# Attention scores computed in column groups of 32, and streamed weights issued at other steps, in a four-layer prompt kernel

## The chip, the cores and the metric

The kernel runs on one core of one Trainium2 chip. The metric is the device time of one execution in microseconds. The time of the kernel before is the median of three runs.

## The reference

Four layers, A, B, A, B, each added to the residual stream `x` of 2048 tokens by 640 features. Only layer A is touched by the change.

```python
# layer A, on the layer-normed x: 64 segments of 32 tokens, one after the other
mem = mem0                                   # 8 memory rows x 640
for s in range(64):
    h = concat([mem, x[32*s : 32*s+32]])     # 40 rows
    q, k, v = h @ Wq, h @ Wk, h @ Wv         # 32 heads of 192
    scores = q @ k.T * 192**-0.5             # 40 x 40 per head, masked
    p = softmax(scores)
    o = (p @ v) @ Wo                         # back to 40 x 640
    mem = o[:8]                              # carried to the next segment
    outs.append(o[8:])
```

Layer B is a linear attention over all 2048 tokens, with learned feature maps.

## The kernel before

**Segments and rounds.** `A_pre` computes, for all segments at once, what does not depend on the memory: keys, queries and values of the last 8 tokens of each segment, stored in DRAM (`kqb_d`, `vb_d`). `A_chain` then walks the 64 segments in order, since each needs the memory rows of the one before. In a segment the 32 heads are worked off in `NR` = 4 rounds of 8 heads, in rising order in even segments and falling order in odd ones. The instruction order is written out by hand for all engines; nothing is rescheduled. Of the 40 rows of a segment, 32 (8 memory rows and the first 24 tokens) go through the chain's projections, as `hT`, 128 x 5 x 32.

**One round** (`n` is 0 to 3), in TensorE's order: the projection of the queries of the next round (`project`, L1154: five steps over the contraction, each with four matmuls into four 32-column tiles of the array, 32 stationary columns and 384 moving ones); the scores (`scores`, L1191) with the exponential on ScalarE (`weigh`, L1273, into `E`); in round 1 some products with Wo (`wo_round`, L1263); the projection of the next round's keys; `attend` (L1204, `ps_o`) and `attend_tails` (L1217, `ps_t`), which multiply E with the values; in round 2 eight more products with Wo; the projection of the next round's values. After round 3's scores come the rest of the products with Wo, the sum that makes the next `hT` (L1453, L1455), and the next segment.

**The scores.** `QK` holds keys and queries of eight heads as 128 x (2, 8, 80): of the 80 columns 64 belong to the 32 rows of two heads (turned there by VectorE, L1174, from `raws`, which ScalarE fills from PSUM, L1169) and 16 to the last tokens of the two heads (copied in by GpSimd, L1130, from `kqb`). `KT` and `QT` are its two halves. Two matmuls add up to one 80 x 80 block of `S`; a round has four blocks, so eight matmuls, each with 80 stationary columns on the whole array. There is one `QK`, so VectorE and GpSimd write the next round's columns after the scores have read these. Round 3's keys are turned in two halves.

**Streamed weights.** Most of Wq, Wk, Wv and Wo lies in SBUF. Seven pieces of 384 KB (3 of Wq, 2 of Wk, 2 of Wv) are held in slots that two rounds share, and `wo_both`, four pieces of 320 KB, holds rows 4 to 11 of Wo for the first or the last round. After round 0 has used a slot, `project` puts the load that refills it for round 3 into the list `held`; `load_both` adds the four Wo pieces in round 1, the one with rows 4 and 5 last. Round 3 reads rows 6 to 11 first, then 0 to 5. `release` takes the first load from the list and issues it on SP's queue, with a wait on one given matmul, so that few loads are under way at a time. Which matmul that is stands in the table `PACE`: for a projection (`"Q"`, `"K"` or `"V"`, round) the contraction step after which one load is released:

```python
if PACE.get((m, n)) == i:
    self.release(last)
```

Of the kernel before, what the change touches and what calls it, by code (L numbers as in the profile page):

```python
# [22 lines left out]

VH = 194

PACE = {("Q", 0): 0, ("K", 0): 1, ("V", 0): 3, ("Q", 1): 3, ("K", 1): 1, ("V", 1): 1, ("Q", 2): 1, ("K", 2): 3, ("V", 2): 3,
        ("Q", 3): 3, ("K", 3): 3}

STEPS = (2, 6)

# [92 lines left out]
class Kernel:  # L123
# [934 lines left out]
    def A_chain(self, xn_dram, at_dram, li, load_slot, piece, late_wo, load_both, wo, low):  # L1058
        nc, tc, KC, NSEG = self.nc, self.tc, self.KC, self.NSEG
        scale = float(self.Dh) ** -0.5  # L1060
        NR = 4
        with tc.tile_pool(name=f"A{li}_ch", reuse_waits="tile", bufs=1) as sp, \
# [4 lines left out]
            KT, QT = QK[:, 0], QK[:, 1]  # L1067
# [69 lines left out]
            def project(hT, ps, m, n, s, steps):  # L1137
# [3 lines left out]
                for i in steps:  # L1141
# [14 lines left out]
                    if n == 0 and b >= KC - ns:  # L1156
                        self.held.append(lambda b=b: load_slot(m, order[NR - 1], b))
                    if PACE.get((m, n)) == i:
                        self.release(last)
# [25 lines left out]
            def scores():  # L1185

                S = pop.tile([P, 512], F32, name="ps_s", tag="s")
                for x in range(2):
                    for c in range(4):
                        c0 = 160 * x + 80 * (c // 2)  # L1190
                        nc.tensor.matmul(S[0:80, c0:c0 + 80], lhsT=KT[:, 4 * x + c, :], rhs=QT[:, 4 * x + c, :],  # L1191
                                         start=(c % 2 == 0), stop=(c % 2 == 1), skip_group_check=True)
                return S

            pair = [None]
# [72 lines left out]
            def weigh(E_before=None):  # L1268
                S = scores()
                if E_before is not None:  # L1270
                    attend_tails(E_before, 2)
                E = sp.tile([P, 320], BF16, name="E", tag="E")
                nc.scalar.activation(out=E[0:80, 0:320], in_=S[0:80, 0:320], func=ACT.Exp, scale=scale)  # L1273
                return E
# [276 lines left out]
```

## Time and profile before

| | us |
|---|---|
| median of three runs | 3175.91 (3167.55 to 3177.78) |
| profiled execution | 3169.9 |
| its span, first to last instruction | 3168.0 |
| of which the two A chains | about 1189 and 1192 |
| TensorE busy | 2993.8 (95%) |
| VectorE, ScalarE, GpSimd busy | 2184.4, 1906.3, 1392.8 |
| DMA engines' mean busy share within the A chains | 78% |

PE is TensorE's matmuls, PEld its weight loads, DVE VectorE, ACT ScalarE, POOL GpSimd, SP SyncE. L1154 is line 1154 of the kernel. Matmuls are pipelined, and their ends are modelled: a start-to-start distance says more than the length of one. Times are microseconds from the start of the span unless marked ns. The granted TensorE clock was 0.992 of full speed over the span. A row of a group gives line, engine, operation, tiles (out<-in), shape and count, then busy time and mean ns of one, then the idle time ahead of these instructions and what ended most of it; "issue" there means nothing that the profile shows.

### The profile page before, as it was taken

What the parts mean: (1) busy time and instruction counts of PE and PEld (TensorE: products, weight loads), DVE (VectorE), ACT (ScalarE), POOL (GpSimd) and SP (SyncE); (2) the same over time, 40 slices, a digit from 0 to 9 for tenths busy, and PEclk for the clock granted to TensorE, in tenths of its full rate; (3) what the DMA queues carried; (4) which work ended last, traced back from release to release, by engine and by line L of the source; (5) the groups of instructions that cost most, each with busy time, mean ns of one, the idle gap of its engine ahead of it and who ended that gap; (6) DMA issues with size and microseconds to landing.
All of it is one profiled execution on the core that took longest, in us unless ns stands there. A gap on an engine that the chain in (4) does not pass through costs nothing.

```text
span 3168.0 us, 141538 instructions
## 1 busy us (share of the span) xinstructions
PE 2993.8 (95%) x59586; PEld 1920.6 (61%) x59586; DVE 2184.4 (69%) x5426; ACT 1906.3 (60%) x4536; POOL 1392.8 (44%) x2872
## 2 busy tenths in 40 slices
PE   8789999999999999899999999999999999998999
PEld 7656666666666665555377566666666666665553
DVE  5467777777777777656644677777777777776565
ACT  3356666666666666646433566666666666666453
POOL 3255555555555555430122555555555555554300
PEclk9999999999999999999999999999999999999999
DMA  9977777877877877840268777777877777778300
GB/s 377 340 263 257 261 248 251 265 257 250 272 252 251 267 256 246 288 166 1 103 246 320 257 255 246 263 264 245 264 259 249 255 261 255 246 259 287 130 1 34
DMA packets 338873, 749.67 MB, mean 237 GB/s; under 512 B 68874, under 2 KB 115330, under 8 KB 335166
## 3 DMA queue, kind: packets, MB, share of 16 engines
q1 hardware_dynamic: 267998, 636.89, 58.3%
q0 software_dynamic: 69376, 100.10, 10.9%
q8 instruction: 469, 7.68, 1.0%
q10 hardware_dynamic: 864, 3.64, 0.3%
q14 instruction: 166, 1.36, 0.1%
HBM read 670.77 MB, written 78.01 MB: 236 GB/s over the span
## 4 chain that ended last, share of the span: by engine, by line
PE 76%; DVE 8%; DMA 6%; issue 5%; ACT 3%; POOL 2%; ACTq 0%; DVEq 0%; SPq 0%; POOLq 0%
PE ps_qk_k L1154 13%; PE ps_qk_q L1154 13%; PE ps_v L1154 12%; PE ps_w L1263 11%; PE ps_s L1191 6%; PE ps_pre L985 4%; PE ps_o L1204 3%; PE kv L1506 2%; DVE raws L1453 2%; ACT raws L1234 2%; DVE hT L1455 2%; PE ps_pq L517 2%; PE ps_t L1217 1%; PE ps_wo L466 1%; DVE QK L1377 1%
## 5 line engine op out<-in xcount | busy, mean ns | idle before, releaser
L1154 PEld LDWEIGHTS <-hT 128*32 128x32 bf16 x30720 | 787.1, 96 | 461.0 <-DVE hT L1455 78.7
L1174 DVE STREAM_TRANSPOSE QK<-raws 128x512 bf16<-128x512 bf16 (+1 forms) x1152 | 730.0, 642 | 219.3 <-ACT raws L1169 163.7
L1130 POOL COPY QK<-kqb 64x192 bf16<-64x192 bf16 x1024 | 349.5, 341 | 486.6 <-PE ps_s L1191 254.1
L1154 PE MATMUL ps_qk_q<-arena,hT 128*32 128x384 bf16 x10240 | 511.3, 327 | 41.4 <-DVE hT L1455 25.6
L1154 PE MATMUL ps_qk_k<-arena,hT 128*32 128x384 bf16 x10240 | 510.1, 328 | 3.0 <-ACT E L1273 1.4
L1169 ACT ACTIVATE raws<-ps_qk_k 128x512 bf16<-128x512 f32 (+1 forms) x640 | 313.5, 510 | 254.0 <-PE ps_qk_k L1154 243.5
L1234 ACT ACTIVATE raws<-ps_o,under 128x192 bf16<-128x192 f32 x1024 | 373.8, 420 | 121.9 <-DVE under L1228 102.5
L1154 PE MATMUL ps_v<-arena,hT 128*32 128x384 bf16 x8192 | 428.4, 326 | 4.0 <-issue 3.0
L1169 ACT ACTIVATE raws<-ps_qk_q 128x512 bf16<-128x512 f32 x512 | 305.7, 597 | 166.6 <-PE ps_qk_q L1154 153.1
L1134 POOL DMA_DIRECT2D Vp<-vb x512 | 257.9, 504 | 316.6 <-PE ps_t L1217 210.7
L1123 POOL DMA_DIRECT2D kqb<-kqb x512 | 292.4, 571 | 69.7 <-POOL QK L1130 59.4
L1191 PEld LDWEIGHTS <-QK 128*80 128x80 bf16 x4096 | 196.0, 121 | 184.9 <-issue 153.8
L1183 DVE CAST Vp<-ps_v 64x384 bf16<-64x384 f32 x512 | 286.3, 559 | 24.5 <-ACT Vp L1181 8.7
L1263 PE MATMUL ps_w<-arena,under 128*32 128x320 bf16 x6144 | 280.6, 300 | 9.5 <-DMA arena<-wo_rows 4.1
L1191 PE MATMUL ps_s<-QK 128*80 128x80 bf16 x4096 | 253.4, 209 | 21.8 <-POOL QK L1130 13.6
L1181 ACT ACTIVATE Vp<-ps_v 64x384 bf16<-64x384 f32 x512 | 246.4, 481 | 35.1 <-PE ps_v L1154 33.6
L1273 ACT ACTIVATE E<-ps_s 80x320 bf16<-80x320 f32 x512 | 217.7, 425 | 42.8 <-PE ps_t L1217 28.6
L985 PEld LDWEIGHTS <-arena 128*128 128x128 bf16 x1920 | 187.9, 98 | 31.0 <-issue 4.7
L1119 POOL DMA_DIRECT2D attn<-under x128 | 91.3, 713 | 262.0 <-DVE under L1115 223.5
L1112 ACT ACTIVATE raws<-ps_w 64x160 f32<-64x160 f32 x256 | 76.6, 299 | 201.1 <-DVE raws L1453 199.6
L1204 PE MATMUL ps_o<-Vp,E 80*32 80x193 bf16 x4096 | 180.3, 248 | 10.2 <-issue 5.7
L1263 PEld LDWEIGHTS <-under 128*32 128x32 bf16 x6144 | 147.2, 96 | 41.6 <-issue 9.8
(167 smaller groups left out, 4360.5 us busy)
## 6 DMA issues: line engine op xcount, KB each, us to landing
arena<-wo_rows SPq DMA_DIRECT2D x560, 320.0 KB, 4.8
arena<-in_A_Wq_dram SPq DMA_DIRECT2D x427, 384.0 KB, 4.5
arena<-in_A_Wk_dram SPq DMA_DIRECT2D x298, 384.0 KB, 5.6
arena<-in_A_Wv_dram SPq DMA_DIRECT2D x290, 384.0 KB, 5.9
kqb<-kqb POOLq DMA_DIRECT2D x512, 48.0 KB, 4.3
kqb<-arena POOLq DMA_DIRECT2D x14, 1536.0 KB, 9.7
Vp<-vb POOLq DMA_DIRECT2D x512, 24.2 KB, 3.8
otb<-otb POOLq DMA_DIRECT2D x256, 48.0 KB, 4.0
```

Source lines behind the costliest of these rows:

```text
L985: nc.tensor.matmul(ps[:, T * i:T * i + T], lhsT=w[b][:, P * c:P * c + P], rhs=xBT[:, b, :], start=(b == 0), stop=(b == KC - 1))
L1123: nc.gpsimd.dma_start(out=kqb[:], in_=self.kqb_d[r, :, s, :])
L1130: nc.gpsimd.tensor_copy(out=o, in_=kqb[h, :].rearrange("p (x c q) -> p x c q", c=3, q=16))
L1134: nc.gpsimd.dma_start(out=Vs[n % 2][64:80, :], in_=self.vb_d[s // 8, r].rearrange("g (t s) x f -> s (g t) (x f)", s=8)[s % 8])
L1154: last = nc.tensor.matmul(o, lhsT=hT[:, b, :], rhs=rhs, start=(i == 0), stop=(i == KC - 1), tile_position=(0, 32 * g), skip_group_check=True)
L1169: nc.scalar.activation(out=raw[:, c], in_=ps[:, c], func=ACT.Copy)
L1174: nc.vector.transpose(out=o, in_=i)
L1183: nc.vector.tensor_copy(out=o, in_=i)
L1191: nc.tensor.matmul(S[0:80, c0:c0 + 80], lhsT=KT[:, 4 * x + c, :], rhs=QT[:, 4 * x + c, :], start=(c % 2 == 0), stop=(c % 2 == 1), skip_gro ...
L1204: nc.tensor.matmul(O[G][32 * h:32 * h + 32, VH * G:VH * G + 193], lhsT=E[0:80, 80 * h + 32 * G:80 * h + 32 * G + 32], rhs=V[0:80, VH * h:V ...
L1234: nc.scalar.activation(out=out, in_=i, func=ACT.Copy, scale=rc[G])
L1263: step = nc.tensor.matmul(W[q:q + 32, 0:320], lhsT=OT[i // 6][:, i % 6 // 2, 32 * (i % 2):32 * (i % 2) + 32], rhs=rhs, start=(first and i ...
```

## The change

The eight score matmuls of a round become 24: each is cut along its 80 stationary columns (the keys) into groups of 32, 32 and 16, which go to the column tiles 0, 32 and 64 of the array and to the same partitions of `S`. The moving operand, `QT` with 80 columns, and the sums are as before, in all four rounds.

The table `PACE` gets other steps. Eleven loads are released in a segment, in the same order as before; the n-th load moves from one step to another:

| load | released before after | released now after |
|---|---|---|
| 1 to 3, Wq | Q0 step 0, K0 step 1, V0 step 3 | Q0 step 0, K0 step 2, V0 step 4 |
| 4 and 5, Wk | Q1 step 3, K1 step 1 | K1 step 0, V1 step 1 |
| 6 and 7, Wv | V1 step 1, Q2 step 1 | Q2 step 3, K2 step 1 |
| 8 to 11, Wo | K2 step 3, V2 step 3, Q3 step 3, K3 step 3 | V2 step 1, Q3 step 1, K3 step 1, V3 step 2 |

```diff
-PACE = {("Q", 0): 0, ("K", 0): 1, ("V", 0): 3, ("Q", 1): 3, ("K", 1): 1, ("V", 1): 1, ("Q", 2): 1, ("K", 2): 3, ("V", 2): 3,
-        ("Q", 3): 3, ("K", 3): 3}
+PACE = {("Q", 0): 0, ("K", 0): 2, ("V", 0): 4, ("K", 1): 0, ("V", 1): 1, ("Q", 2): 3, ("K", 2): 1, ("V", 2): 1, ("Q", 3): 1,
+        ("K", 3): 1, ("V", 3): 2}
...
                 for x in range(2):
                     for c in range(4):
                         c0 = 160 * x + 80 * (c // 2)
-                        nc.tensor.matmul(S[0:80, c0:c0 + 80], lhsT=KT[:, 4 * x + c, :], rhs=QT[:, 4 * x + c, :],
-                                         start=(c % 2 == 0), stop=(c % 2 == 1), skip_group_check=True)
+                        for g, m in enumerate((32, 32, 16)):
+                            nc.tensor.matmul(S[32 * g:32 * g + m, c0:c0 + 80], lhsT=KT[:, 4 * x + c, 32 * g:32 * g + m],
+                                             rhs=QT[:, 4 * x + c, :], start=(c % 2 == 0), stop=(c % 2 == 1),
+                                             tile_position=(0, 32 * g), skip_group_check=True)
```

## The prediction

> **What bounds the kernel now.** I read the page first, then the groups by line, then TensorE's timeline of one segment, then the timelines of ScalarE and of the weight queue, and last the landings of the weight loads.
>
> ```profile
> PE 2993.8 (95%) x59586; PEld 1920.6 (61%) x59586; DVE 2184.4 (69%) x5426; ACT 1906.3 (60%) x4536; POOL 1392.8 (44%) x2872
> ...
> PE 76%; DVE 8%; DMA 6%; issue 5%; ACT 3%; POOL 2%; ACTq 0%; DVEq 0%; SPq 0%; POOLq 0%
> ```
>
> TensorE is busy 95% and is 76% of the chain that ended last. The stretches table gives two A chains of 1189 and 1192 us: 64 segments of some 18.6 us each, four rounds to a segment, 512 rounds in all. Only these chains change.
>
> ```profile
> L1191 PEld LDWEIGHTS <-QK 128*80 128x80 bf16 x4096 | 196.0, 121 | 184.9 <-issue 153.8
> ...
> L1191 PE MATMUL ps_s<-QK 128*80 128x80 bf16 x4096 | 253.4, 209 | 21.8 <-POOL QK L1130 13.6
> ```
>
> The first group is the scores' weight loads: 153.8 us of idle time ended by nothing that the profile shows, 0.3 us for each of the 512 blocks. TensorE's timeline (start, length, line, tiles, count) shows it inside one round:
>
> ```profile
> 902.25 0.34 PE L1204 MATMUL ps_o<-Vp,E 80*32 80x193 bf16 x8
> 902.42 0.26 PE L1217 MATMUL ps_t<-Vp,E 80*32 80x193 bf16 x4
> 902.50 0.34 PE L1154 MATMUL ps_v<-arena,hT 128*32 128x384 bf16 x4
> ...
> 903.32 0.99 PE L1154 MATMUL ps_qk_q<-arena,hT 128*32 128x384 bf16 x20
> 904.23 0.50 PE L1191 MATMUL ps_s<-QK 128*80 128x80 bf16 x8
> 904.66 0.73 PE L1263 MATMUL ps_w<-arena,under 128*32 128x320 bf16 x16
> ```
>
> A projection of 20 matmuls takes 0.82 us from its start to the next block's (902.50 to 903.32), five groups of four column tiles at 0.163 us. From 903.32 to 904.66 there are 1.34 us, so a score block costs 0.52. In the trace's single instructions the eight 80-column matmuls start 38 ns apart (0.30 us); 0.10 lie ahead of them (first score weight load 0.255 us after the last projection matmul, where the next group comes after 0.152) and 0.10 to 0.14 behind. These gaps stand only where 32-column blocks give way to 80-column ones and back.
>
> **Scores, the block by itself.** 24 matmuls replace 8 (16,384 more matmuls and as many weight loads). Groups of four column tiles take 0.163 us for 384 columns and 0.083 for 193 (902.25 to 902.42 holds two), that is 0.42 ns a column and 2 ns; 80 columns give 0.036 us for the three tiles of a product and 0.29 for eight. The 16-column tile is in the trace too (ps_t, 80*16) and follows 32-column tiles without a gap. So 0.53 becomes 0.29: 0.24 saved per block, 125 us over 512, if TensorE alone set the time. Bounds for a pair of load and matmul: 2 ns an instruction when it is popped from a full queue; 8.8 ns (56 instructions between two semaphore waits 0.49 us apart) if that were the sequencer's pace, which makes 48 instructions 0.42 us. I take the streaming value since tiles of one group start 3.5 ns apart; the other end would cost 0.16 us a segment, 20 us. The densest long stretch here is 12 matmuls in 0.25 us (902.25 to 902.50), 21 ns each.
>
> The Trainium skill, "TensorE: Matmul & The Clock Gate", section "Wait — 56ns, not 53.3ns?", says that start-to-start never falls below about 25 ns however few columns there are; by that the 24 would take 0.60 us, an estimate, and 512 blocks lose some 35 us. Those 21 ns already lie below it. The same page, "Part 3: Packing small matmuls", says that a weight load overlaps matmuls in flight only in another row group; here all loads use the same rows and still cost nothing between projection groups.
>
> **What of it reaches the path.** Per segment, with the waits of the other engines:
> - Round 0: the block cannot start earlier, since its key transposes end 0.15 us ahead of it (VectorE) in nearly every segment. Only the gap behind goes: 0.11.
> - Round 1: VectorE and GpSimd are done 0.4 and 2 us ahead, and ps_w covers the exponential. All of it: 0.24.
> - Round 2: ScalarE runs without a break from the scaled rows to E:
>
> ```profile
> 906.97 0.73 ACT L1234 ACTIVATE raws<-ps_o,under 128x192 bf16<-128x192 f32 x2
> 907.59 0.48 ACT L1181 ACTIVATE Vp<-ps_v 64x384 bf16<-64x384 f32 x1
> 907.96 0.41 ACT L1247 ACTIVATE raws<-ps_t,under 128x192 bf16<-128x192 f32 x1
> 908.26 0.59 ACT L1169 ACTIVATE raws<-ps_qk_q 128x512 bf16<-128x512 f32 x1
> 908.74 0.43 ACT L1273 ACTIVATE E<-ps_s 80x320 bf16<-80x320 f32 x1
> ```
>
> E ends at 909.17 and ps_o of that round starts at 909.26; over all segments ps_o starts 0.14 us after E, where 0.10 is the least seen. Earlier scores do not make E earlier: 0.03 gained, the rest becomes a wait of ps_o on E.
> - Round 3: the second half of the key transposes ends at 910.68, 0.05 after the block has begun; that chain hangs on ps_o of round 2. 0.19 gained.
>
> Sum 0.57 us a segment, 73 us over 128. GpSimd's copies into QK end a median 0.64 us (a tenth under 0.16) before round 3's scores, which now come up to 0.45 earlier: I put 5 us for that, bounds 0 and 15. TensorE's extra instructions cost nothing by themselves while the streaming value holds.
>
> **Streamed weights.** Each segment reloads seven 384 KB slots and four 320 KB pieces. On SP's queue:
>
> ```profile
> 898.02 2.44 SPq L748 DMA_DIRECT2D arena<-in_A_Wq_dram  x3
> 900.95 1.36 SPq L748 DMA_DIRECT2D arena<-in_A_Wk_dram  x2
> 903.05 1.14 SPq L748 DMA_DIRECT2D arena<-in_A_Wv_dram  x2
> 906.09 3.55 SPq L797 DMA_DIRECT2D arena<-wo_rows  x4
> ```
>
> Seven are issued within 5.8 us. Median time to landing by position, from the landing semaphores: 4.03, 4.50, 4.53, 4.97, 5.55, 5.67, 6.09, then 4.72, 4.66, 4.82, 4.37. That is a queue: with the seventh 5.84 after the first, (6.09 - 4.03 + 5.84)/6 = 1.31 us of service for 384 KB and 2.72 fixed; likewise 0.97 and some 2.65 for the pieces. It gives the positions between to 0.25 us.
>
> The order of the eleven stays; the steps move. An issue follows its matmul group by 0.38 us. Counted from the segment's first matmul, with the gains above, the new issues fall at 0.39, 1.53, 2.67, 4.07, 5.30, 6.45, 7.78 and 8.83, 9.65, 10.75, 12.39. The queue then gives 4.50 for the seventh (the last slot of Wv) and 3.66 for the eleventh (the piece with rows 4 and 5, which the last products of the segment read). Their uses come 4.55 and 3.7 us after issue. Before, they came 6.5 and 5.0 after it, with median slacks of 0.69 and 0.64 us; now both are near nothing, while every other load keeps over 0.5. With the spread of those landings (deviation 0.48 us, taken segment by segment from the trace) the mean stall is 0.30 us a segment, 38 us in all. A piece behind a stall in ps_v has that much more time, so the two do not add. Ends: 0.13 us (17 us) if landings come 0.3 sooner, 0.54 (69 us) if 0.3 later. SP's store of vb waits in the same queue behind the eleventh, but for an eviction 3 us later, so it is not delayed.
>
> **Sum.** 73 - 5 - 38 = 30 us. The profiled execution is 3169.9 us with a span of 3168.0; it would come to about 3140. The median of the runs shown is 6 us higher: 3176 - 30 = 3146, and I give 3145.
>
> **Rivals.**
> - *The pace holds* (0.20). Spread issues shorten the landings more than the queue says, and stalls stay at 10 us or less: 3176 - 73 + 5 + 10 = 3118, down to 3085 if round 2's ScalarE chain also gives way. For it: the share of DMA is 78% in the chains, not full. Against: 4.03 us is the landing of a load with no other in front.
> - *The last slot of Wv is late* (0.18, slower). It is released at step 1 of K in round 2, some 1.9 us later than before, and used at step 4 of V in round 3, 4.55 us after issue. If landings stay above 5.1 us, as for positions 5 to 7 now, the 0.57 gained is gone; at 5.55 the stall is 1.0 and the time 3176 + (1.0 - 0.57) x 128 + 5 = 3236; at 5.2, 3190. For it: those landings are in the trace. Against: they were reached with loads 1 us apart, and the new gaps are 1.1 to 1.6.
> - *Issue-bound tiles* (0.10). If 24 pairs go no faster than the 21 ns each seen, a block costs 0.50 and nearly nothing is saved, while looser timing leaves the loads their slack: 3165 to 3185. The skill's 25 ns would make it about 3210.
> - Forecast (0.52): stalls take 10 to 56 us of the 68 left after GpSimd's 5: 3118 to 3164.
>
> **Numbers.** About 0.3%, 10 us, is what a measurement can tell. Faster: 0.50 of the forecast and 0.20 of the first rival, 0.70; slower: 0.17 of the second and 0.04 of the third, 0.21; within it the rest, 0.09. The range 3085 to 3200 takes in the first rival, the third, and the cheap end of the second; left out is a tenth to a fifth.
>
> **What would show it.** Right: score blocks of 24 that take 0.29 us with no gap either side, the idle time of their weight loads gone from 153.8 to under 30 us; waits of ps_o on E in round 2; waits of ps_v and ps_w on DMA of 20 to 60 us in all where now there are 9; Wv landings near 4.5. Wrong: blocks over 0.4 us (issue), or DMA waits over 80 us (the pace), or under 10 (the gain larger).

## The result and the profile after

The changed kernel takes 3276.93 us (median of four runs) where the kernel before took 3174.4 beside it: a ratio of 1.0333, 95% interval 1.0302 to 1.0364. It is 3.3% slower, where 1% faster was forecast. The profiled execution has a span of 3286.7 us, 118.7 longer.

The page after, with the lines that answer to those of before, and the instruction queue's line (packets, MB, share), first as it stands on the page of before:

```profile
q8 instruction: 469, 7.68, 1.0%
```

```profile
PE 2963.5 (90%) x67778; PEld 2041.0 (62%) x67778; DVE 2180.9 (66%) x5426; ACT 1912.5 (58%) x4536; POOL 1397.0 (43%) x2872
...
q8 instruction: 533, 8.73, 1.1%
...
PE 68%; DMA 12%; DVE 8%; issue 6%; ACT 4%; POOL 1%; SPq 0%; DVEq 0%; ACTq 0%; POOLq 0%
...
L1192 PE MATMUL ps_s<-QK 128*32 128x80 bf16 (+1 forms) x12288 | 251.5, 202 | 37.7 <-issue 21.4
L1192 PEld LDWEIGHTS <-QK 128*32 128x32 bf16 (+1 forms) x12288 | 211.1, 96 | 111.0 <-DVE QK L1174 38.2
```

TensorE is busy for less time (2963.5 us against 2993.8) in a longer span, so work was removed and waiting added. The weight loads of the scores no longer wait 153.8 us for nothing (34.7 us of "issue" are left in the waits). The instruction queue moved 533 packets of 16 KB instead of 469; the trace holds 136,485 instructions of TensorE (weight loads, matmuls and waits), 256 for each packet.

TensorE's timeline of a round in which nothing is late shows what the column groups do (line 1192 is the scores):

```profile
396.85 0.99 PE L1154 MATMUL ps_qk_q<-arena,hT 128*32 128x384 bf16 x20
397.67 0.39 PE L1192 MATMUL ps_s<-QK 128*32 128x80 bf16 x18
397.86 0.31 PE L1265 MATMUL ps_w<-arena,under 128*32 128x320 bf16 x1
397.88 0.25 PE L1192 MATMUL ps_s<-QK 128*32 128x80 bf16 x6
397.95 0.72 PE L1265 MATMUL ps_w<-arena,under 128*32 128x320 bf16 x15
```

The scores follow the projection at its usual 0.82 us, and the next block's groups follow 0.28 us later (one matmul of it, for the column tile that the scores leave free, slips in before them). The single instructions show groups of three 35 ns apart. Two rounds on, in the same segment:

```profile
403.73 0.29 PE L1192 MATMUL ps_s<-QK 128*32 128x80 bf16 x9
405.18 0.29 PE L1192 MATMUL ps_s<-QK 128*32 128x80 bf16 x9 [1.16 <-issue]
405.27 0.26 PE L1219 MATMUL ps_t<-Vp,E 80*32 80x193 bf16 x1
405.28 0.25 PE L1192 MATMUL ps_s<-QK 128*32 128x80 bf16 x6
```

After nine of the 24 matmuls TensorE stands still for 1.16 us, and nothing that the profile follows releases it. Among the DMA packets of the trace there is one of the instruction queue, 16 KB, from 402.94 to 403.83: TensorE goes on 1.35 us after it has landed. That is the pattern to look for. Some of TensorE's longest waits (total us, times, longest us), after:

```profile
PE ps_w L1265 <- issue: 71.4, 67, 2.6
PE ps_qk_k L1154 <- issue: 34.5, 37, 2.1
...
PE ps_w L1265 <- DMA arena<-wo_rows: 22.4, 42, 1.6
...
PE ps_s L1192 <- issue: 21.4, 26, 2.3
...
PE ps_v L1154 <- DMA arena<-in_A_Wv_dram: 11.4, 21, 1.9
PE ps_v L1154 <- issue: 10.2, 18, 1.1
```

and the same of before:

```profile
PE ps_w L1263 <- issue: 13.6, 24, 1.5
...
PE ps_w L1263 <- DMA arena<-wo_rows: 8.1, 12, 1.5
...
PE ps_v L1154 <- issue: 3.0, 8, 0.6
...
PE ps_v L1154 <- DMA arena<-in_A_Wv_dram: 0.6, 1, 0.6
```

To compare kernels I counted, in the A chains of each trace, every distance over 0.33 us between successive matmul starts, less the ordinary 0.152. It is a *late instruction fetch* if TensorE resumes 1.15 to 1.65 us after the last packet of the instruction queue ended, a *late weight* if it resumes within 0.06 us of the landing of a streamed load. The window for fetches was set by eye: in the changed kernel the gaps before ps_qk_k lie 1.28 to 1.53 us (10% to 90%) behind the packet. Some gaps are counted there by chance. Those in neither class (some 100 to 135 us in every kernel) are waits for other engines, VectorE most of all.

The last column of the table needs no window. It counts TensorE's instructions from the start of the trace and takes the gaps that begin at one fixed instruction of every 256. In the changed kernel 194 of all 572 gaps begin there, in both chains at position 193; the other gaps are spread over all positions. (Where 18 matmul records are missing from a trace, position 175 of the second chain is the same instruction.) So TensorE stops at the end of the instructions that it holds: these are late fetches, and of the 30 and 15 us that the window gives e5 and e8 most is chance.

| kernel | median us | ratio to before | late fetch, us (times) | late weight, us (times) | stops at the fixed instruction, us (times) |
|---|---|---|---|---|---|
| before | 3172 | | 50 (89) | 27 (31) | 41 (68) |
| changed | 3277 | 1.033 | 207 (221) | 54 (94) | 193 (194) |
| e1 new scores, old steps | 3270 | 1.030 | 222 (254) | 18 (26) | 211 (230) |
| e2 old scores, new steps | 3241 | 1.022 | 39 (73) | 108 (164) | 29 (45) |
| e3 before + empty matmuls, bunched | 3325 | 1.048 | 167 (200) | 11 (18) | 160 (179) |
| e6 before + empty matmuls, spread | 3288 | 1.036 | 107 (164) | 16 (24) | 98 (137) |
| e5 as e1, nothing streamed | 3031 | 0.955 | 30 (75) | 4 (3) | 7 (9) |
| e9 as e1, no Wo pieces streamed | 3192 | 1.006 | 161 (212) | 18 (19) | 147 (166) |
| e8 before, nothing streamed | 3096 | 0.975 | 15 (32) | 2 (5) | 2 (3) |
| e10 new scores in round 0 alone | 3176 | 1.000 | 74 (120) | 29 (35) | 60 (88) |
| e4 new scores in round 1 alone | 3183 | 1.004 | 101 (141) | 22 (29) | 94 (119) |
| e11 new scores in round 3 alone | 3209 | 1.011 | 86 (124) | 29 (37) | 83 (108) |

For the changed kernel the account nearly closes: late fetches +157, late weights +28, and a gain of 65 to 72 us (e8 against e5, below) come to 113 to 120; the span grew by 118.7, the median by 102.5. The granted clock was 0.985 of full speed in this profiled execution against 0.992 before, which is worth 23 us at most (an estimate, as if TensorE's clock set the whole time); e1 loses nearly as much at 0.991.

### The profile page after: what moved, and what is told of

It is laid out like the page before. It is cut to its first block, busy times and chain, and to the rows that moved or that the text cites. A ratio compares the mean times of both kernels' runs of the same rounds, so it can differ in the third digit from the quotient of the medians.

```text
span 3286.7 us, 157795 instructions
## 1 busy us (share of the span) xinstructions
PE 2963.5 (90%) x67778; PEld 2041.0 (62%) x67778; DVE 2180.9 (66%) x5426; ACT 1912.5 (58%) x4536; POOL 1397.0 (43%) x2872
## 4 chain that ended last, share of the span: by engine, by line
PE 68%; DMA 12%; DVE 8%; issue 6%; ACT 4%; POOL 1%; SPq 0%; DVEq 0%; ACTq 0%; POOLq 0%
PE ps_qk_q L1154 12%; PE ps_qk_k L1154 12%; PE ps_v L1154 10%; PE ps_w L1265 9%; DMA arena<-wo_rows 6%; PE ps_pre L985 5%; DMA arena<-in_A_Wv_dram 4%; PE ps_s L1192 4%; PE ps_o L1206 3%; PE kv L1508 2%; DVE raws L1455 2%; ACT raws L1236 2%; PE ps_wo L466 2%; PE ps_pq L517 1%; DVE hT L1457 1%
## 5 line engine op out<-in xcount | busy, mean ns | idle before, releaser
L1154 PEld LDWEIGHTS <-hT 128*32 128x32 bf16 x30720 | 925.9, 97 | 438.9 <-issue 117.2
L1154 PE MATMUL ps_qk_k<-arena,hT 128*32 128x384 bf16 x10240 | 552.2, 328 | 34.8 <-issue 34.5
L1154 PE MATMUL ps_qk_q<-arena,hT 128*32 128x384 bf16 x10240 | 525.3, 329 | 46.5 <-DVE hT L1457 22.8
L1154 PE MATMUL ps_v<-arena,hT 128*32 128x384 bf16 x8192 | 449.0, 327 | 20.4 <-DMA arena<-in_A_Wv_dram 11.4
L1265 PE MATMUL ps_w<-arena,under 128*32 128x320 bf16 x6144 | 310.3, 301 | 36.1 <-issue 31.2
L1192 PE MATMUL ps_s<-QK 128*32 128x80 bf16 (+1 forms) x12288 | 251.5, 202 | 37.7 <-issue 21.4
L1192 PEld LDWEIGHTS <-QK 128*32 128x32 bf16 (+1 forms) x12288 | 211.1, 96 | 111.0 <-DVE QK L1174 38.2
L1265 PEld LDWEIGHTS <-under 128*32 128x32 bf16 x6144 | 187.1, 97 | 47.0 <-issue 40.2
L1206 PE MATMUL ps_o<-Vp,E 80*32 80x193 bf16 x4096 | 195.2, 251 | 16.1 <-issue 5.7
```

The source lines that it names most:

```text
L1154: last = nc.tensor.matmul(o, lhsT=hT[:, b, :], rhs=rhs, start=(i == 0), stop=(i == KC - 1), tile_position=(0, 32 * g), skip_group_check=True)
L1192: nc.tensor.matmul(S[32 * g:32 * g + m, c0:c0 + 80], lhsT=KT[:, 4 * x + c, 32 * g:32 * g + m], rhs=QT[:, 4 * x + c, :], start=(c % 2 == 0) ...
L1206: nc.tensor.matmul(O[G][32 * h:32 * h + 32, VH * G:VH * G + 193], lhsT=E[0:80, 80 * h + 32 * G:80 * h + 32 * G + 32], rhs=V[0:80, VH * h:V ...
L1265: step = nc.tensor.matmul(W[q:q + 32, 0:320], lhsT=OT[i // 6][:, i % 6 // 2, 32 * (i % 2):32 * (i % 2) + 32], rhs=rhs, start=(first and i ...
```

## The experiments

**Each half alone.** Theory A: TensorE runs out of instructions. Theory B: the release steps make the loss. e1 keeps the table of before:

```diff
 PACE = ...            # as before
+                        for g, m in enumerate((32, 32, 16)):   # scores as changed
```

> The new scores with the release steps of the kernel before. Theory A (TensorE runs out of instructions: 16 KB fetches that resume it some 1.4 us after they land, more often since a score block now takes 48 instructions): the fetch-like stalls stay near the 210 us of the changed kernel (52 before), DMA waits near the 17 us of before, and the time is 3240 to 3280. Theory B (the release steps make the loss): fetch-like stalls matter little and the time is about 3100, the 73 us gained.

Measured: 3270.08 us, ratio 1.0301 (1.0276 to 1.0327). A holds: late fetches 222 us, late weights 18. Of its waits:

```profile
PE ps_w L1265 <- issue: 46.5, 61, 1.6
PE ps_s L1192 <- issue: 39.8, 45, 2.3
PE ps_qk_k L1154 <- issue: 35.4, 34, 2.8
...
PE ps_w L1265 <- DMA arena<-wo_rows: 7.9, 11, 1.7
```

e2 is the other half: the new table, with the eight matmuls of 80 columns.

> The scores of before with the new release steps. Theory A: fetch-like stalls stay near 52 us; the eleventh load is used 3.9 us after issue and lands after 4.4, so DMA waits rise by 0.3 to 0.6 us a segment, 40 to 75 us: 3215 to 3250. Theory B: the whole loss is here, and more, since nothing is gained: 3280 or above.

Measured: 3241.04 us, ratio 1.0224 (1.0195 to 1.0254). A's range again, and the release steps are a loss of their own, 2.2%:

```profile
PE ps_w L1263 <- DMA arena<-wo_rows: 52.1, 94, 1.6
...
PE ps_v L1154 <- DMA arena<-in_A_Wv_dram: 21.8, 43, 1.1
```

Late weights rise by 81 us, late fetches do not. B's claim that the whole loss is here is refuted by e1. In the changed kernel the same steps cost only 28 us of late weights, probably because time lost to instructions is time in which weights land.

**Instructions without the scores.** e3 adds 16 matmuls of one moving column behind each unchanged score block, into columns of `S` that nothing reads:

```diff
+                for i in range(16):
+                    g = i % 4
+                    nc.tensor.matmul(S[32 * g:32 * g + 32, 400:401], lhsT=hT[:, 0, :], rhs=hT[:, 0, 0:1],
+                                     start=True, stop=True, tile_position=(0, 32 * g), skip_group_check=True)
```

> The kernel before with 16 added matmuls of one moving column behind each score block, into columns of S that nothing reads: the same number of TensorE instructions as in the changed kernel, no gap removed, release steps of before. Theory A: fetch-like stalls rise from 52 to 150 to 220 us; with 0.04 to 0.1 us of TensorE time a block the kernel takes 3290 to 3400. Theory B: only those 20 to 50 us: 3195 to 3225.

Measured: 3325.01 us, ratio 1.0482 (1.0452 to 1.0512), in theory A's range; late fetches 167 us, and 0.11 us of TensorE's time a block. Instructions that compute nothing bring back three quarters of the added stalls, with no change of the scores or the steps. e6 spreads as many over the projections (65 a segment against 64), and writes unused columns of `ps_w`. Unlike e3's, these matmuls alter the kernel's result, probably because `ps_w` holds sums that are still open; e6 tells of time alone.

> The kernel before with as many empty one-column matmuls as e3 (65 a segment against 64), but spread one or two to a step over the projections instead of 16 behind each score block, into columns of ps_w that nothing reads. If the number of instructions makes the stalls, the fetch-like stalls are 150 us or more, as in e3 (167); if their bunching does, they stay under 100. TensorE's own time for them is open, 15 to 80 us.

Measured: 3287.59 us, ratio 1.0360 (1.0343 to 1.0377), late fetches 107 us. Neither answer holds alone: spread instructions add half the stalls that bunched ones do (57 us against 117), so number and bunching both count.

**Why a fetch is late.** e5 is e1 without the streamed loads of all but the last segment:

```diff
+                if self.dry:          # set in segments 0 to 62: mark the slot, load nothing
+                    return None
```

> As e1 (new scores, release steps of before), but the eleven streamed loads of every segment but the last are left out in both A layers, so round 3 multiplies with the weights that the slots hold already. If instruction fetches come late because weight packets stand ahead of them, the fetch-like stalls fall from 222 us to under 80 and the time to 3090 to 3120. If a fetch simply takes its 2.4 us and is asked for too late for so dense an instruction stream, the stalls stay above 150 us and the time near 3240, lower than e1 by its 18 us of DMA waits and little else.

Measured: 3030.58 us, ratio 0.9551 (0.9534 to 0.9568), late fetches 30 us, only 7 of them at the fixed instruction, with the same 533 fetches. The time is 60 us below its range: the late fetches and weights that went come to 206 of the 240 us, and the rest is not accounted for. So the fetch of 2.4 us is not too slow in itself; it is late when loads of weights are under way. e9 streams the seven slots but not the Wo pieces:

> As e5, but only the four Wo pieces of a segment are left out and the seven 384 KB slots are loaded: two thirds of the streamed bytes. If fetches wait behind the packets of loads, the fetch-like stalls lie between 30 (nothing streamed) and 222 (all), 80 to 160 us, and the time between 3031 and 3270; stalls in the rounds 0 and 1, where the slot loads still are in flight, stay, and those after round 2 go.

Measured: 3191.95 us, ratio 1.0060 (1.0041 to 1.0078), late fetches 161 us, a hair above the expected bound, and only in part where expected. Behind round 3's scores 36 us are left (e1: 86). From round 1's scores to round 3's 126 us stay (e1: 134), and half of these fall after round 2's scores, where they should have gone: 63 us (e1: 72) with a mean 1.0 streamed load under way in place of 4.2.

The traces show why. The fetch of the next 256 instructions never starts sooner than some 20 instructions before TensorE passes the fixed instruction ahead of them, and TensorE stops 256 instructions after that passing if they are not there. Between round 2's scores and round 3's there are only 162 instructions, so a fetch that is missed there was due before, when e9 still has a mean 3.7 loads under way. In e1 the median packet starts 1.1 to 1.3 us after the passing when at most two streamed loads are under way then, 1.6 us with three, 2.3 with four and 2.6 with five; in e5 it is 0.6 us. The packet itself takes 1.0 to 1.1 us each time. Loads under way delay the start of a fetch, not its transfer.

e8 takes the streamed loads from the kernel before, to see the gain of the column groups free of both waits.

> The kernel before with the streamed loads left out as in e5 (scores of 80 columns, release steps of before; round 3 multiplies with the weights that the slots hold). Without waits on loads and with few late fetches the two score forms stand side by side: e5 at 3031, and this one 73 us above it if the columns gain what the traces say, 3095 to 3115. Its own fetch-like stalls should be under 30 us where before has 50.

Measured: 3095.84 us, ratio 0.9751 (0.9724 to 0.9778), late fetches 15 us. e5 stands 65 us below it: that is what the column groups are worth when little else is late. The median segment takes 17.38 us in e5 and 17.94 here, 0.56 less, which makes 72 us over 128.

**Column groups in one round.** `scores` takes the round and cuts only in that one (32 added instructions a segment), with the steps of before:

```diff
-                S = scores()
+                S = scores(n in (1,))      # (0,) in e10, (3,) in e11
```

> Column groups only in round 1, where the whole 0.24 us of a block reaches the path; release steps of before; 32 added instructions a segment instead of 128. Theory A: a gain of 31 us less a quarter of the 158 us of added stalls if they grow in proportion, 3180 or so, 3145 to 3160 if they grow faster than the count. Theory B: 3143.

Measured: 3183.38 us, ratio 1.0043 (1.0026 to 1.0060). It is the 3180 given for theory A with stalls in proportion, not theory B's 3143. Late fetches grew by 52 us for a quarter of the instructions (172 for all of them, in e1), rather more than in proportion, and outweigh the 31 us gained.

> Column groups in round 0 only, release steps of before. In all runs so far hardly any stall falls between round 0's scores and round 1's (3 us of over 200), where few loads are in flight. If the place of the instructions matters, the 14 us that round 0 gains stay and the added stalls are under 10 us: 3160 to 3170, faster than before. If each 16 added matmuls a segment cost their stalls wherever they stand, as in round 1 (52 us), the time is 3195 to 3215.

Measured: 3175.64 us, ratio 1.0002 (0.9989 to 1.0015): no difference. Neither expectation holds. The stalls did not follow in the same round (2 us), but later ones grew: 74 us in all, 24 more, which eats the gain. The reason given for the round was wrong: a mean 4.5 streamed loads are under way between its scores and the next, as many as in the two stretches that follow. But fewer than 256 instructions lie between them (194), so the fetches that could be missed there were due before round 0's scores; behind round 3's scores only 1.4 loads are under way on average.

> The same in round 3 only, where 0.1 to 0.2 us of a block reaches the path (13 to 25 us) and half of the Wo loads are in flight. Stalls of 20 to 50 us added behind round 3's scores: 3175 to 3205, not faster than before.

Measured: 3208.67 us, ratio 1.0111 (1.0094 to 1.0128). Late fetches 86 us, 62 of them behind round 3's scores (29 before). Not faster, as expected, and a little worse than the range.

**Earlier release on the kernel before.** e7 moves the last four releases to step 1:

```diff
-("Q", 2): 1, ("K", 2): 3, ("V", 2): 3, ("Q", 3): 3, ("K", 3): 3
+("Q", 2): 1, ("K", 2): 1, ("V", 2): 1, ("Q", 3): 1, ("K", 3): 1
```

> The kernel before with its last four releases at step 1 instead of step 3 of K and V in round 2 and of Q and K in round 3, 0.33 us earlier each; scores of before. The last Wo piece then has 5.3 us instead of 5.0 to land: DMA waits before ps_w fall from 13 us to under 6, unless the queue takes the difference. 3163 to 3172, at or within what can be told from before.

Measured: 3174.98 us, ratio 1.0002 (0.9988 to 1.0016). No difference, where 3163 to 3172 was expected; the late weights stayed at 26 us (27 before), so the fall in waits did not come.

No version ran faster than the kernel before with all its work done.

## Why the prediction was wrong

**The score block: right.** Groups 35 ns apart (0.036 predicted), 0.28 us a block (0.29), no gap on either side. The rule of 25 ns from start to start in the Trainium skill ("TensorE: Matmul & The Clock Gate", "Wait — 56ns, not 53.3ns?") does not hold here, where one matmul follows another on a different column tile: 24 matmuls start within 0.26 us, 11 ns each. On one and the same tile they are 35 ns apart. The rule in the same page of the Trainium skill ("Part 3: Packing small matmuls") that loads overlap only across row groups is not borne out either, since the loads of these column groups, all on the same rows, stay hidden.

**What of it reaches the path: the sum right, its parts not.** The shortest segment of e1 takes 17.38 us, that of before 17.93: some 0.56 saved, 0.57 predicted. Over the kernel, e8 less e5 gives 65 us (73 predicted). By rounds, in medians of e8 less e5, counted from round 0's scores to the start of each round's ps_o, round 0 saves 0.07 (0.11 predicted), round 1 0.33 (0.24), round 2 nothing (0.03), round 3 0.07 (0.19), and 0.09 comes in the stretch to the next round 0, which has no term. That they add up so well is luck. Round 2's new wait is there, and the same wait in round 0, which was not foreseen:

```profile
PEld L1206 <- ACT E L1275: 66.8, 222, 0.7
```

This is ps_o's weight load waiting for the exponential, after: 33 us in round 2, 33 in round 0.

**"TensorE's extra instructions cost nothing by themselves": this step failed.** It weighed the pace at which the array takes instructions, and never asked how they arrive. The rows were there in the kernel before: 469 packets of the instruction queue, and 27 us of TensorE's idle time in the A chains ended by "issue", in gaps of up to 1.5 us, far longer than the 0.10 to 0.14 us beside a score block. The term put at 0, with 20 us as its far end, measured 157 us in the changed kernel (late fetches 207 less 50) and 172 in e1. The rival "issue-bound tiles" looked in the right place for the wrong thing: blocks do not run slower; TensorE stops, in a block or elsewhere, when its instructions run out.

**The pace: the mechanism right, two sizes off.** 38 us of stalls were predicted and 28 measured, but this is luck. The queue gave 4.50 us to the seventh load and 3.66 to the eleventh; they landed after a median of 4.78 and 4.45. The eleventh had 4.37 before: a wider spacing of the issues did not shorten it. With the old scores, where TensorE stops less for instructions, the steps cost 69 us (e2). The slower rival had the wrong load as the worst: ps_w's waits for the Wo piece (52.1 us in e2) exceed ps_v's for the last slot of Wv (21.8).

**The range** left out any loss above 3200: the slower times that were priced came from the pace and from issue-bound tiles, none from the fetch of instructions.

**What stays open.** The time at which a fetch is asked for is not in the trace, so where it waits until its packet starts, behind the packets of the loads or elsewhere, cannot be told. The Trainium skill, "Runtime: NRT & Kernel Launch", section "Instruction fetch mechanics", says that instructions come in blocks of 16 KiB on a queue of their own and that crossing from one to the next is mostly hidden. The block size agrees with the trace; hidden it is in e5 and e8, and not under streamed weights.

## What to carry to other kernels

Count instructions as traffic: where TensorE is near its limit and weights are streamed, 16 KB for every 256 instructions have to be fetched while the weights load, and a change that trades few long matmuls for many short ones has to be priced in fetches too. Read idle time ended by "issue", compare its end with the packets of the instruction queue, and see whether the stops fall on the same instruction of every 256, before adding instructions. A release that is moved later must be checked against landings as measured, not as they would be in a thinner queue.

## What the runs showed of the hardware

- In the stalls counted, a 16 KB instruction packet takes 0.9 to 1.4 us, and TensorE resumes a median 2.4 to 2.5 us after its start, streamed weights or not. What changes is how late the packet starts, and so how often and how long TensorE stops at the fixed instruction: 194 times for 1.0 us in the changed kernel, 9 times for 0.8 us in e5.
- In the A chains no packet of any run starts more than 22 instructions before TensorE passes the fixed instruction, and TensorE stops 256 further on when the packet has not landed: at most one packet is fetched ahead. The median packet starts 32 instructions past the fixed one in e5 and 120 past it in e1.
- A stop shows about 256 instructions after its fetch was due, and so not always where loads are under way. In the changed kernel 3 us of late fetches fell between round 0's scores and round 1's, with 3.4 streamed loads under way on average, 44 and 41 in the next two stretches, and 122 behind round 3's, with 1.7.
- With four column tiles in use by the neighbours and three by a block, the next block's matmul for the idle tile starts before the block has ended (397.86 above).
